# Reading all early expert rows at once, ahead of the next weight pieces, in a fused attention and expert-routing kernel

## The chip, the cores and the metric

The kernel runs on one core of a Trainium2 chip. The metric is the device time of one execution in microseconds; the kernel before was run three times. A separate execution under the hardware profiler gave the profile and the trace; all stretches and starts below are microseconds from the start of that profiled execution.

The engines go by these names: PE is TensorE (matmuls; PEld its weight loads), DVE is VectorE, ACT is ScalarE, POOL is GpSimd, SP is SyncE. In this kernel SP issues plain transfers (inputs, and the reads of routed rows), and POOL issues the indirect scatters and all weight transfers.

## The reference, cut to what matters

A linear attention without softmax, normalized per head, feeds a mixture of experts that sends each token to one expert:

```python
kv  = einsum('bhsd,bhse->bhde', k, v)             # 8 batches, 8 heads, 576 tokens, 64 wide
out = einsum('bhsd,bhde->bhse', q, kv)
out = out / sqrt(mean(out * out, -1) + 1e-6) * g_norm
x   = out.transpose(0, 2, 1, 3).reshape(4608, 512)
logits = x @ w_gate                                # 8 experts
e      = argmax(logits);  gate = softmax(logits)[e]
y[token] = gate * (relu(x[token] @ w1[e]) @ w2[e]) # w1: 512x1024, w2: 1024x512
```

## The kernel before: the parts that matter here

The tokens are worked in four pairs of batches (`j` = 0 to 3, nine tiles of 128 tokens each). For each tile TensorE makes the outputs (`o_mm`, tag `O`), ScalarE squares, VectorE reduces (`o_red`), ScalarE makes the reciprocal root (`o_nrm`), and VectorE scales into the row buffer `xrow` and the logits `lhat` (`o_x`), one tile behind. Every few tiles a `route` gives each token a slot in its expert's region of a DRAM table `x_slots`, and GpSimd scatters the rows there. Where a route is done in pieces (`chunks`), the last pieces are three tiles long.

```python
chunks = {0: [(0, 9)], 1: [(0, 9)], 2: [(0, 6), (6, 9)], 3: [(0, 3), (3, 6), (6, 9)]}
EARLY, EARLY_TILES = 3, 3

def route(j, t0, t1):                 # a generator: one step for each call of job()
    ...  # step 1: logits, maximum, one-hot (VectorE); ids into xrow (GpSimd)
    yield
    yield                             # step 2: nothing
    ...  # step 3: exp (ScalarE); ranks by matmul (rps, TensorE)
    yield
    ...  # step 4: positions, 1/sum (VectorE), then for each tile:
    for t in range(T):
        w = nc.gpsimd.indirect_dma_start(out=xs_views[9 * j + t0 + t], ...)   # scatter of rows
    yield
```

Experts 0, 1 and 2 have an early group each: the first 3 x 128 slots of the expert, which are filled from pairs 0 to 2 alone. After the last route of pair 2 a further job, `early_rows`, starts the reads of these groups. A group's rows are read by SyncE in four transfers of 96 KB, plus its gates and token ids (`gi`); such a read waits until the scatters have landed.

```python
def early_rows():
    ...                               # four small VectorE operations
    groups[0].fetch()
    yield
    yield
    groups[1].fetch()
    yield

def fetch(self):
    r0 = self.e * N + 128 * self.k0
    pool, bufs = (P_fe, 2) if self.table == "early" else (late["pool"], 3)
    self.xl = pool.tile([128, self.n // 32, 128], I16, tag="xl", bufs=bufs, name="xl")
    for i in range(4):
        r = nc.sync.dma_start(self.xl[32 * i : 32 * i + 32], ...)
        ...
    r = nc.sync.dma_start(self.gi[:, 0 : self.K], tail)
```

A group is then transposed and scaled on VectorE (`xpose`), and goes through `stage1` (eight times: four matmuls, ReLU on ScalarE into `hT`) and `stage2` (per 128 rows: eight matmuls into `yp`, gated on VectorE into `y`, scattered to the output by GpSimd). Early groups have three `y` buffers and two PSUM buffers each for `hp` and `yp`.

```python
def ffn():                            # one unit() = one stage1(f) or one stage2(k)
    to_fetch = list(groups[2:])
    ...
    for f in range(8):
        cur.stage1(f)
        ...
        if f == 1 or f == 5 and cur.K == SLOT_TILES:
            w_step()
        if f >= 4 and f % 2 == 0 and (f - 4) // 2 < parts:
            nxt.xpose((f - 4) // 2, parts)
        yield
    for k in range(cur.K):
        cur.stage2(k)
        if k % 2 == 1:
            w_step()
        ...
        yield
```

`w_step` issues the next of four weight pieces per expert on GpSimd's queue (two of w1, two of w2; float32 in DRAM, float16 in SBUF, 512 KB written each), in the order of the experts. After the attention `final_rows` starts pad scatters (`pads`, zero rows into unused slots), which GpSimd issues between the outputs, and which the reads of the later groups wait for.

The loop over the batches; `b` = 7 has pair 3's tiles 0 to 3, `b` = 8 (`B`) its tiles 4 to 8. A tile's `job()` calls run the waiting routes one step each.

```python
for n, t in enumerate(tiles):
    do_fill(1 if n == 0 and b < B else per - 1)
    job()
    tile_step(j, t)
    do_fill(1)
    o_nrm(j, t)
    job()
    if b == 6 and n >= 3 or b == 7 and n != 2 or b == B:
        w_step()
    if b == 7 and n == 3:
        w_step()
    if b == B and n >= 2:
        unit()
        unit()
```

Of the kernel before, what the change touches and what calls it, by code (L numbers as in the profile page):

```python
# [22 lines left out]
B, H, S, DH = 8, 8, 576, 64  # L23
# [11 lines left out]
EARLY = 3  # L35
# [10 lines left out]
def kernel(  # L46
# [94 lines left out]
    for j in range(4):  # L141
        for t0, t1 in chunks[j]:
            n = n_route
# [11 lines left out]
    P_fe = ctx.enter_context(tc.tile_pool(name="pearly", bufs=1))  # L155
# [13 lines left out]
    late = {}  # L169
# [61 lines left out]
    def id_index(name, ctr, ne, nk):  # L231
        badi = P_const.tile([128, ne, nk], I32, tag="badi" + name, name="badi" + name)
        nc.vector.tensor_tensor(
            badi, _bc(cv["srank"][:, 0:nk], 1, ne), _bc(ctr[:, 0:ne], 2, nk), op=ALU.is_ge
        )
        nc.vector.tensor_scalar(badi, badi, BIG, None, op0=ALU.mult)
        rows[name] = badi
# [5 lines left out]
    def disjoint(ins, others):  # L243
        for o in others:
            tc.declare_no_dep(ins, o, reason="other rows of the slots")


    def early_rows():
        ctr = P_const.tile([128, 8], F32, tag="cnt_x")
        b0 = base[len(routed)]  # L250
        nc.vector.tensor_tensor(ctr, b0, cv["ebase"], op=ALU.subtract)
        id_index("early", ctr, EARLY, EARLY_TILES)
        nc.vector.tensor_tensor(b0, b0, cv["efloor"], op=ALU.max)
        groups[0].fetch()
        yield
        yield
        groups[1].fetch()
        yield

    def final_rows():  # L260
# [6 lines left out]
    class Group:  # L267
# [28 lines left out]

        def fetch(self):
            r0 = self.e * N + 128 * self.k0
            pool, bufs = (P_fe, 2) if self.table == "early" else (late["pool"], 3)
            self.xl = pool.tile([128, self.n // 32, 128], I16, tag="xl", bufs=bufs, name="xl")  # L300
            for i in range(4):
                r = nc.sync.dma_start(
                    self.xl[32 * i : 32 * i + 32],
                    xs.ap()[r0 : r0 + self.n, 128 * i : 128 * i + 128].rearrange(
                        "(g b) w -> b g w", b=32
                    ),
                )
                disjoint(r.ins, [p for g, p in pad_ins if g is not self])
                read_ins.append(r.ins)
            self.gi = P_fe.tile([128, SLOT_TILES, 4], I16, tag="gi", bufs=4, name="gi")  # L310
            tail = xs.ap()[r0 : r0 + self.n, D:ROW].rearrange("(k p) w -> p k w", p=128)
            r = nc.sync.dma_start(self.gi[:, 0 : self.K], tail)
            disjoint(r.ins, [p for g, p in pad_ins if g is not self])
            read_ins.append(r.ins)
# [219 lines left out]
    groups = [Group(i, i, 0, EARLY_TILES) for i in range(EARLY)]  # L534
# [3 lines left out]
    def ffn():  # L538
        order = list(groups)
        side = []  # L540
        to_fetch = list(groups[2:])

        def fetch_up_to(n):
            while to_fetch and groups.index(to_fetch[0]) <= n:
                if to_fetch[0].table not in rows:
                    return
                to_fetch.pop(0).fetch()

        n = 0
        while n < len(order):  # L550
            cur = order[n]
            real = groups.index(cur) if cur in groups else -1
            nxt = groups[real + 1] if 0 <= real < len(groups) - 1 else None
            parts = 0 if nxt is None else 2 if nxt.K == SLOT_TILES else 1
            while w_todo and any(e == cur.e for e, _ in w_todo):
                w_step()
            if real == 0:
                cur.xpose()
            if real == EARLY:
                side.append(dyn_tables())  # L560
            for f in range(8):
                cur.stage1(f)
                if f == 0 and real >= 0:
                    fetch_up_to(real + (3 if real >= EARLY else 2))
                    if EARLY - 1 <= real < len(groups) - 4:
                        groups[real + 4].pads()
# [4 lines that stand above are left out]
                if f == 5:  # L571
                    cur.slot_ids()
                if f == 5 and cur.e == E - 1:
                    nc.gpsimd.drain()
                if f == 3 and cur.e == EARLY + 1:
                    spill = SpillGroup(tabs[0], slice(0, 1), out_views[E * SLOT_TILES])
                    spill.fetch()
                    n_more.append(
                        nc.values_load(
                            tabs[0][4][0:1, 0:1], min_val=0, max_val=MAXDYN - 1,  # L580
                            skip_runtime_bounds_check_because="the count of tiles is bounded",
                        )
                    )
                    order.insert(len(order) - 1, spill)
                for g in side:
                    next(g, None)
# [5 lines that stand above are left out]
                if k == 0 and real >= 0:  # L592
                    fetch_up_to(real + 2)
                if k == 3 and cur.e == E - 2:
                    spill.xpose()
                for g in side:
                    next(g, None)
                yield
            n += 1

    steps = ffn()

    def unit(n=1):
# [7 lines left out]
    with tc.tile_pool(name="pattn", bufs=1) as PA:  # L611
# [72 lines left out]
        def z_copy(b):  # L684
            zs[b] = PA.tile([128, 4, 64], F32, tag="z", bufs=2, name=f"z{b}")
            nc.scalar.copy(zs[b], kvps[b])
# [153 lines left out]
        def job():  # L840
            while jobs:
                try:
                    next(jobs[0])
                    return
                except StopIteration:
                    jobs.pop(0)
# [27 lines left out]
        for b in range(B + 1):  # L874
            fill = []
            if b < B:
                for u in range(2):
                    if b > 0:
                        fill.append(("kv", u))
                    for g in range(3 * u, 3 * u + 3):  # L880
                        fill.append(("t", g))
                    if b == 0:
                        fill.append(("kv", u))
                fill.append(("fold", 0))
            tiles = []
            if b > 0:
                j = (b - 1) // 2
                tiles = list(range(4)) if b % 2 else list(range(4, 9))
            per = (len(fill) + len(tiles) - 1) // len(tiles) if tiles else len(fill)

            def do_fill(n):
                for _ in range(n):
                    if not fill:
                        return
                    kind, x = fill.pop(0)
                    if kind == "kv":
                        kv_mm(b, x)
                        if b == 0:
                            load(2, x)
                        if x == 1:  # L900
                            z_copy(b)
                    elif kind == "t":
                        t_mm(b, x)
                        if x % 3 == 2:
                            if 0 < b < B - 2:
                                load(b + 2, x // 3)
                            if 2 * b + x // 3 in range(2, 2 + EARLY):
                                clear_early(2 * b + x // 3 - 2)
                    else:
                        fold_mm(b)  # L910
                        x_copy(b)

            if not tiles:
                do_fill(99)
# [4 lines that stand above are left out]
                do_fill(1)  # L919
                o_nrm(j, t)  # L920
                job()
                if b == 6 and n >= 3 or b == 7 and n != 2 or b == B:
                    w_step()
                if b == 7 and n == 3:
                    w_step()
                if b == B and n >= 2:
                    unit()
                    unit()
            do_fill(99)
# [49 lines left out]
```

## Time and profile before

| | |
|---|---|
| device time, three runs | 316.79, 319.02, 319.94 us; median 319.02 |
| profiled execution | 337.4 us, mean granted TensorE clock 0.888 |
| busy: PE, DVE, ACT, POOL | 268.3, 154.4, 121.3, 146.6 us |
| output matmuls of the attention (line 734) | to 160.0 us |
| first matmul of an early group (line 365) | at 152.3 us |

Three things help to read the views below. A timeline line is start, length, engine, source line, operation, what it writes and reads, how many were merged, and in brackets the idle time just before it with what ended it. SP lines (SPq) are issues, not transfers: the data moves later. In the table by stretch, each engine has its busy time and a count of instructions, and the last three numbers are the granted TensorE clock as a share of full speed, the mean busy share of the 16 DMA engines (it can come out a little over 1), and GB/s. The profiled execution is about 18 us longer than the timed ones; lengths in it are to be read with that in mind.

### The profile page before, as it was taken

The numbers are of one execution on the slowest core, as the hardware profiler recorded it, in microseconds if no ns is written. First come the engines' busy times: TensorE is split into PE (matmuls) and PEld (weight loads), VectorE is DVE, ScalarE is ACT, GpSimd is POOL, SyncE is SP. The second block draws the span as 40 slices with busy tenths as digits, with TensorE's granted clock in tenths as the row PEclk, the third lists the DMA queues.
The fourth block names the chain that finished last, engine by engine and source line by source line (L and its number), as shares of the span: only waits on it lengthen the run. The fifth ranks groups of instructions, "written<-read, shape, count | busy, mean of one in ns | idle before, by whom it ended". The sixth has DMA issues, their size and how long they took to land. (4 is left out here: it accounts for less than half of the span.)

```text
span 337.4 us, 6833 instructions
## 1 busy us (share of the span) xinstructions
PE 268.3 (80%) x2599; PEld 179.8 (53%) x2599; DVE 154.4 (46%) x397; ACT 121.3 (36%) x324; POOL 146.6 (43%) x186
## 2 busy tenths in 40 slices
PE   2789997399839849528597799779799999998991
PEld 1678785287628738424242355445446565654740
DVE  1015674137704645665661419775337282723031
ACT  2236664057505535323322043322414242332510
POOL 8400004600370074351457677777776362623132
PEclk9999999569955896757898799798999999999997
DMA  7999999939980329999922979999999997982012
GB/s 217 340 366 367 381 377 378 384 118 331 277 298 3 64 82 174 187 216 181 223 83 92 195 130 218 193 172 201 205 182 275 224 232 162 207 201 113 3 62 86
DMA packets 63346, 69.17 MB, mean 205 GB/s; under 512 B 31736, under 2 KB 48314, under 8 KB 63312
## 3 DMA queue, kind: packets, MB, share of 16 engines
q0 software_dynamic: 14496, 33.79, 44.8%
q1 hardware_dynamic: 48672, 34.79, 34.9%
q8 instruction: 21, 0.34, 0.4%
q10 hardware_dynamic: 144, 0.14, 0.4%
q14 instruction: 13, 0.11, 0.1%
HBM read 71.77 MB, written 20.79 MB: 274 GB/s over the span
## 5 line engine op out<-in xcount | busy, mean ns | idle before, releaser
L373 ACT ACTIVATE hT<-hp 128x320 f16<-128x320 f32 (+3 forms) x136 | 53.4, 426 | 114.2 <-PE hp L365 95.8
L365 PE MATMUL hp<-xT,w1e 128*128 128x320 f16 (+2 forms) x512 | 79.8, 309 | 15.7 <-DVE xT L327 7.0
L381 PE MATMUL yp<-w2e,hT 128*128 128x512 f16 x320 | 76.6, 397 | 4.6 <-DVE y L386 2.1
L365 PEld LDWEIGHTS <-w1e 128*128 128x128 f16 x512 | 51.1, 100 | 43.6 <-issue 22.5
L386 DVE TENSOR_SCALAR y<-yp,gi 128x512 f32<-128x512 f32 x40 | 29.8, 750 | 82.1 <-PE yp L381 75.8
L389 POOL DMA_INDIRECT out_dram<-y,idv x40 | 40.4, 1009 | 59.1 <-DVE y L386 44.9
L381 PEld LDWEIGHTS <-hT 128*128 128x128 f16 x328 | 32.9, 101 | 45.3 <-issue 9.8
L829 POOL DMA_INDIRECT x_slots<-xrow,posi x36 | 35.4, 983 | 49.9 <-issue 42.7
L734 PE MATMUL ops<-kvx,qT 64*128 64x72 f32 (+1 forms) x640 | 48.2, 302 | 4.9 <-issue 3.2
L747 DVE TENSOR_REDUCE ms<-sq 128x8 f32<-128x512 f32 x36 | 24.6, 684 | 58.7 <-ACT sq L743 49.9
L734 PEld LDWEIGHTS ops<-kvx,qT 64*128 64x128 f32 (+1 forms) x640 | 41.2, 205 | 12.7 <-issue 8.2
L677 PE MATMUL kvps<-mk,mv 128*64 128x64 f32 x640 | 31.8, 258 | 16.8 <-issue 11.8
L677 PEld LDWEIGHTS kvps<-mk,mv 128*64 128x64 f32 x640 | 27.5, 168 | 21.1 <-issue 18.9
L665 PE MATMUL tps<-ctile,mq 128*128 128x128 f32 x144 | 28.0, 331 | 12.3 <-DMA mq<-in_q_dram 6.3
L286 POOL DMA_INDIRECT x_slots<-zrow,padall x31 | 30.7, 989 | 9.4 <-issue 8.8
L743 ACT ACTIVATE sq<-ops 128x512 f32<-128x512 f32 x36 | 21.6, 599 | 35.1 <-PE ops L734 21.9
L759 DVE TENSOR_TENSOR xrow<-ops,rs 128x512 f16<-128x512 f32 x36 | 24.7, 685 | 14.3 <-ACT rs L752 12.9
L795 POOL COPY xrow<-tokc 128x3 int32<-128x3 int32 x12 | 2.4, 200 | 59.2 <-DVE xrow L759 59.2
L665 PEld LDWEIGHTS tps<-ctile,mq 128*128 128x128 f32 x144 | 18.5, 164 | 16.3 <-ACT qT L666 6.8
L666 ACT COPY qT<-tps 128x384 f32<-128x384 f32 x48 | 22.1, 473 | 12.1 <-PE tps L665 12.1
L322 DVE STREAM_TRANSPOSE xT<-xl 128x1280 int16<-128x1280 int16 (+2 forms) x16 | 24.0, 1503 | 2.7 <-DMA xl<-x_slots 2.7
L327 DVE TENSOR_SCALAR xT<-xT,g 128x320 f16<-128x320 f16 (+2 forms) x64 | 17.4, 335 | 0.6
(104 smaller groups left out, 140.9 us busy)
## 6 DMA issues: line engine op xcount, KB each, us to landing
mq<-in_q_dram SPq DMA_DIRECT2D x16, 576.0 KB
w1e<-in_moe_w_dram POOLq DMA_DIRECT2D x16, 512.0 KB
w2e<-in_moe_w_dram POOLq DMA_DIRECT2D x16, 512.0 KB
mk<-in_k_dram SPq DMA_DIRECT2D x16, 320.0 KB
mv<-in_v_dram SPq DMA_DIRECT2D x16, 320.0 KB
mk<-in_k_dram SPq DMA_DIRECT2D x16, 256.0 KB
mv<-in_v_dram SPq DMA_DIRECT2D x16, 256.0 KB
xl<-x_slots SPq DMA_DIRECT2D x20, 160.0 KB
```

Source lines behind the costliest of these rows:

```text
L286: p = nc.gpsimd.indirect_dma_start(out=self.pad_views[k], out_offset=IndirectOffsetOnAxis(ap=pad[:, self.e, self.k0 + k : self.k0 + k + 1] ...
L365: nc.tensor.matmul(hp, self.w()[0][:, kk].rearrange("p (m j t) -> p m t j", t=2, j=128)[:, f // 2, f % 2], self.xcols(kk, s), start=(kk == 0),
L373: nc.scalar.activation(self.hT[:, f, s : s + self.step], hp, ACTF.Relu)
L381: nc.tensor.matmul(yp, self.hT[:, f, k * 128 : (k + 1) * 128], self.w()[1][:, f // 2, f % 2, :], start=(f == 0), stop=(f == 7),)
L386: nc.vector.tensor_scalar(y, yp, self.gate(k), None, op0=ALU.mult)
L389: nc.gpsimd.indirect_dma_start(out=self.views(k), out_offset=IndirectOffsetOnAxis(ap=self.ids[:, k : k + 1], axis=0), in_=y, in_offset=Non ...
L665: nc.tensor.transpose(ps[:, c, :], src[:, 128 * m : 128 * m + 128], cv["ident"])
L677: nc.tensor.matmul(kvps[b][64 * y : 64 * y + 64, 2 * u + a, :], main["v", b, u][:, 2 * y + a, c, :], main["k", b, u][:, 2 * y + a, c, :], ...
L734: nc.tensor.matmul(ps[p0 : p0 + 64 * n, y, o0 : o0 + 72], qT[b][hs, a, blk // 2 : blk // 2 + n, :].rearrange("d c p -> d (c p)"), kvx[b][h ...
L747: nc.vector.reduce_sum(mss[j, t], sq, axis=AXX)
L759: nc.vector.tensor_tensor(xr[:, 0:D].bitcast(F16).rearrange("p (u y a d) -> p y u a d", u=2, y=2, a=2), xv.rearrange("p y (u a) d -> p y u ...
L829: w = nc.gpsimd.indirect_dma_start(out=xs_views[9 * j + t0 + t], out_offset=IndirectOffsetOnAxis(ap=posi[:, t : t + 1], axis=0), in_=xrow[ ...
```

## The change

The reads of all three early groups are issued together, in one step, right behind the last scatters of pair 2; the row buffer `xl` of the early groups gets a third copy so that they need not wait for each other. In `b` = 7 each tile runs three job steps instead of two, so the routes there are done sooner. The weight pieces that stood beside the reads (tile 3 of `b` = 7 had two, tile 0 of `b` = 8 one) are not issued there any more: by the end of the attention eight pieces have been issued instead of eleven, and the others follow with the groups. The units of the experts start one tile earlier (`n >= 1` in `b` = 8). It is meant to bring the first groups' rows in sooner, without weight transfers in their way.

```diff
@@ early_rows
-        groups[0].fetch()
-        yield
-        yield
-        groups[1].fetch()
+        for n in range(EARLY):
+            groups[n].fetch()
         yield
@@ Group.fetch
-            pool, bufs = (P_fe, 2) if self.table == "early" else (late["pool"], 3)
+            pool, bufs = (P_fe, 3) if self.table == "early" else (late["pool"], 3)
@@ ffn
-        to_fetch = list(groups[2:])
+        to_fetch = list(groups[EARLY:])
@@ the loop over batches
-                if b == 6 and n >= 3 or b == 7 and n != 2 or b == B:
+                if b == 6 and n >= 3 or b == 7 and n <= 1 or b == B and n >= 1:
                     w_step()
-                if b == 7 and n == 3:
-                    w_step()
-                if b == B and n >= 2:
+                if b == 7:
+                    job()
+                if b == B and n >= 1:
                     unit()
                     unit()
```

In the order of the instructions this moves the following. On GpSimd's queue the last scatters of pair 2 stand behind one w2 piece instead of two and ahead of one w2 piece instead of two w1 and one w2; expert 1's pieces stand behind the first scatters of pair 3, and expert 2's last piece behind the first pad scatters and five outputs. On VectorE the transpose of group 0 stands behind tile 5's reduction (before: behind tile 6's and a route's first step). On TensorE the last route's rank matmuls stand behind the first two outputs of group 0 (before: ahead of all three).

## The prediction

> **What bounds the kernel now.** I first read the shares on the page, then the table of busy time by stretch for the second half, then the waits of TensorE between 120 and 215 us, and last the timelines of SyncE, VectorE, GpSimd and TensorE round the longest of these waits. The chain of waits is of no use here: it ends after one piece, so the path has to be put together by hand. Rows of the stretches (start and end, length, busy time and count of PE, PEld, DVE, ACT, POOL, then granted clock, DMA share, GB/s):
> ```profile
> 118.00:138.40 20.40, 14.57 (x228) 12.36 (x223) 9.33 (x32) 8.40 (x23) 13.10 (x17) 0.83 0.66 140
> 138.40:152.30 13.90, 4.43 (x46) 4.03 (x38) 10.25 (x32) 3.83 (x12) 5.14 (x9) 0.52 1.08 198
> 152.30:163.80 11.50, 9.78 (x68) 5.48 (x67) 7.22 (x20) 5.43 (x14) 3.97 (x5) 0.84 1.05 192
> 249.00:300.00 51.00, 50.70 (x307) 29.91 (x306) 26.13 (x52) 18.37 (x48) 24.50 (x29) 1.00 1.02 218
> ```
> From 249 us on TensorE is busy for 50.7 of 51 us: a microsecond won ahead of this is kept if the feeders keep pace. The hole is 138.4 to 152.3: TensorE works 4.43 of 13.9 us, at a granted clock of 0.52, while the DMA share is 1.08. What ended its waits there (total, times, longest):
> ```profile
> PE hp L365 <- DVE xT L327: 7.0, 1, 7.0
> PE rps L806 <- DVE ohb L793: 4.6, 2, 2.8
> ```
> The 7.0 us are the first matmul of early group 0, which waits for its transposed rows. Who makes those rows late (SyncE's reads; GpSimd's scatters and weight pieces; VectorE's transpose):
> ```profile
> 139.81 2.66 SPq L302 DMA_DIRECT2D xl<-x_slots  x4
> 145.23 3.97 SPq L302 DMA_DIRECT2D xl<-x_slots  x4
> 135.43 0.97 POOL L829 DMA_INDIRECT x_slots<-xrow,posi  x1 [0.30 <-issue]
> 136.39 1.18 POOL L202 DMA_DIRECT2D w1e<-in_moe_w_dram  x2
> 137.66 0.75 POOL L207 DMA_DIRECT2D w2e<-in_moe_w_dram  x1
> 150.11 1.78 DVE L322 STREAM_TRANSPOSE xT<-xl 128x1536 int16<-128x1536 int16 x1 [1.69 <-DMA xl<-x_slots]
> ```
> Group 0's reads are issued at 139.81, once the last scatter of pair 2 (issued 135.43) has landed, and the transpose starts at 150.11: 10.3 us for 384 KB. Between lie three weight pieces, put on GpSimd's queue just ahead. The DMA view of 139.8 to 143.3 us has this queue line alone:
> ```profile
> q0 software_dynamic: 190, 0.71, 105.2%
> ```
> In the first 3.5 us after their issue no packet of the rows (queue 1) moved; the weights held all engines. From 143.3 to 146 the rows got 192 packets, and only from 146 to 152 the rest, two groups together.
>
> **What the Trainium skill says.** DMA: Bandwidth & Descriptors, section "Queues, rings and completion order", says that each DMA engine takes turns between the queues that have work, packet by packet. The trace agrees for 143.3 to 146 (223 weight packets beside 192 of rows): a 256-byte row packet waits its turn behind a 4 KB weight packet. TensorE: Matmul & The Clock Gate, "What's actually happening", says that an idle window of about 3.4 us halves the clock; the clock of 0.52 in the hole agrees, and the first group's 8 matmuls after it took 2.78 us where 8 later ones took 1.46. Perfetto Trace Analysis, "Tensor Engine Instruction", says that the profile's matmul ends are modelled; so I take group lengths by differences of starts.
>
> **The change part by part.**
>
> 1. *Reads without weights beside them.* Before, five weight pieces stand round pair 2's last scatters (two w2 ahead, two w1 and one w2 behind); after, one w2 ahead and one behind. Scatters: the routing step that makes their positions comes after tile 1's reduction instead of ahead of tile 2, about 1 us earlier (one `o_x` and one reduction, 0.69 + 0.26 + 0.69 us, fall behind it, less the wait for the reduction). Landing: before, the scatter packets stood behind two w2 pieces; a w2 piece is 256 packets of 0.173 us on 16 engines, 2.8 us, so some 1 us more is won. I put the reads at 138 us (139.81). Rows then meet one w2 piece at most. A later, undisturbed read shows the cost: group 3's reads were issued at 184.03 and mostly moved by 187.5 to 188. With 4 issues (2.66 us), some 3 us of packets and the completion, rows of group 0 land near 143.5 instead of 150.
>
> 2. *But the transpose is in VectorE's order.* The units start one tile earlier (`n >= 1`), so the transpose stands behind tile 5's reduction. Before, that reduction ran at 143.98 to 144.67; now the second half of a route (seven operations, 144.58 to 145.77: 1.2 us) stands ahead of it, but overlaps waits of 0.6 and 0.8 us. Transpose from about 144.8, then 1.78 and four scalings 1.27: rows ready at about 147.8. The first matmul moves from 152.3 to 147.8, **4.5 us**; the wait is not gone, about 5 us of it is left, so the clock stays low there.
>
> 3. *What was moved behind it.* Tile 6's output matmuls (about 1.1 to 1.5 us) were done ahead of 152.3 and now come behind: **-1.3 us**. In return, the 2.8 us wait of TensorE at 163.8 to 166.6 for the last route's one-hot goes: in the new order the first two outputs of group 0 (16 matmuls, 3.5 us) stand ahead of that route's matmuls. **+2.8 us.** Sum at group 1's first matmul: 4.5 - 1.3 + 2.8 = 6.0 us (173.3 to about 167.3).
>
> 4. *Weights come later against the compute.* Three pieces fewer are issued by the end of the attention (8 instead of 11); every later piece slips by about one early group. Expert 1: four pieces issued at about 147 to 151; at 2.6 us (w1: 128 packets of 0.325 us on 16 engines) and 2.8 us each they take 11 us, landed by about 162, wanted at 167: hidden. Expert 2's last w2 piece is the tight one. It now stands in GpSimd's queue behind the last three scatters, six pad scatters and outputs 4 and 5. An indirect scatter takes 0.98 us and 0.30 between: 1.29 each. The last scatters end at about 174.3 (176.1 before: they stand behind three outputs now); a w2 piece 0.8; six pads 7.8, to 183; two outputs 2.6; the piece ends its issue at 186.6 and lands some 4 us later (2.8 of packets), at 190.5. TensorE, 6 us early, wants it after group 1 (two stages, 6.4 + 5.2 as group 2's starts at 191.61, 197.99 and 203.16 show), group 2's first stage (6.4) and four matmuls: 167.3 + 18.0 + 0.9 = 186.2. **A new wait of about 4.3 us, over half of the gain.**
>
> 5. *GpSimd's queue.* From 176 to 249 us it runs nearly back to back (43.66 of 58 us busy from 191 to 249, plus 0.3 between each two). It decides when `y` buffers (three in the early groups) come free. Its end of the first pads moves from 186.4 to about 183, 3 us, so it can't pass on much more than that. Weights for experts 3 to 7 keep over 15 us between issue and use: expert 4's, issued 213 to 228 before, are wanted at 254.
>
> 6. *The third row buffer* removes group 2's wait for a free buffer (its reads went out at 153.48, right after group 0's transpose ended, for a transpose at 175): hidden before, worth nothing.
>
> Sum: 6.0 - 4.3 = 1.7 us by TensorE's path, about 3 us by GpSimd's; and if the wait for the weights is missing, up to 6. I choose **3 us: 316.0**, nearer to the lower two. One caution: the profiled execution took 337.4 us, the timed ones 319. In the profile TensorE's results come 3 to 5 us late at several places (VectorE waited 10.0 us for the first output of group 1, until 188.31), and I counted group lengths there from undisturbed groups.
>
> **The rivals.**
> - *The bound passes fully to the weights or to GpSimd.* If the pads and outputs end no earlier, expert 2's last piece and the `y` buffers eat all 6 us: 319, or 321 if DMA traffic makes the piece land 2 us later still. For it: the unbroken GpSimd queue, and the DMA share of 1.00 from 191 to 249. Against: the last scatters do come earlier.
> - *The hole closes further and the weights arrive in time.* With the DMA engines quiet (share 0.48 from 173.3 to 191 before) the piece may land sooner, and a shorter hole may leave the clock at full: then 6 to 7 us, 312 to 313.
> - *The read was hidden anyway.* If VectorE or the clock, not the rows, set the start of group 0, the gain is 1 us. Against: the 1.69 us wait of the transpose for the rows just ahead of 150.11, after which nothing else was missing.
>
> **Range and chances.** The terms that pull against each other are each some 3 us uncertain; the three times before spread over 3.2 us. Range 311.5 to 320.0. Over 2% faster needs under 312.6, the second rival nearly whole: 0.15. Over 2% slower needs 325.4: 0.04. Within 2%: 0.81.
>
> **What would show it.** (a) Group 0's rows issued at about 138 and its transpose about 5 us earlier than 150.1; (b) a wait for xT of about 5 instead of 7.0 us; (c) no wait of 2.8 us for the one-hot ahead of group 0's outputs; (d) a wait in group 2's second stage for expert 2's w2, some 2 to 4 us, or none, if I am wrong on the weights; (e) the first pads end about 3 us sooner; (f) from group 3 on the same lengths. Wrong would I be above all if (d) is absent (then faster) or if the later weights are missed again at expert 3 (then slower).

## The result and the profile after

The kernel before took 317.90 us in this comparison (median of 4 runs, 316.76 to 319.94), the changed one **306.06 us** (4 runs, 305.54 to 307.45). The ratio is 0.9627, with an interval of 0.9559 to 0.9695: 12 us gained, where 3 were foretold. The execution under the profiler has a span of 304.1 us.

The waits of TensorE from 90 to 200 us in the changed kernel (total, times, longest, in us):

```profile
PE yp L379 <- DMA w2e<-in_moe_w_dram: 7.3, 1, 7.3
PE hp L363 <- DVE xT L325: 6.8, 2, 6.6
PE rps L804 <- DVE ohb L791: 3.7, 2, 2.9
```

The wait for group 0's rows (`xT`) is 6.6 us and the new wait for expert 2's `w2` is there, 7.3 us. By these lines alone the change should have lost: 7.0 before against 6.6 + 7.3 now. What answers to the reads and the weight pieces in the timelines of SyncE, GpSimd and VectorE (start, duration, engine, tiles, count, and in brackets the idle time before):

```profile
114.83 2.04 SPq L300 DMA_DIRECT2D xl<-x_slots  x4
117.43 2.14 SPq L300 DMA_DIRECT2D xl<-x_slots  x4
120.21 2.20 SPq L300 DMA_DIRECT2D xl<-x_slots  x4
...
109.20 0.77 POOL L207 DMA_DIRECT2D w2e<-in_moe_w_dram  x1
120.37 1.18 POOL L202 DMA_DIRECT2D w1e<-in_moe_w_dram  x2
123.45 1.43 POOL L207 DMA_DIRECT2D w2e<-in_moe_w_dram  x2
...
119.73 1.78 DVE L320 STREAM_TRANSPOSE xT<-xl 128x1536 int16<-128x1536 int16 x1 [2.35 <-DMA xl<-x_slots]
```

All three groups' reads are issued within 8 us, the next weight pieces come behind those of the first, and the transpose starts 4.9 us after its reads are issued (10.3 before). But these starts are 25 to 30 us earlier than those of the profile before (139.81 and 150.11), which no part of the change can do: the attention ahead of them is the same work. Here lies the key to the missing 9 us. The profiled execution of before took 337.4 us, the timed ones 317 to 319. In it TensorE crept in the attention; the stretch from 57 to 70 us (busy time and count of PE, PEld, DVE, ACT, POOL, then granted clock, DMA share, GB/s), first in that execution:

```profile
57.00:70.00 13.00, 6.67 (x56) 4.46 (x58) 2.24 (x4) 2.59 (x7) 6.84 (x8) 0.63 0.92 335
```

and in a second profile of the same kernel, whose execution took 315.76 us (run e13_before below):

```profile
57.00:70.00 13.00, 12.37 (x247) 10.92 (x248) 8.55 (x18) 9.25 (x27) 6.71 (x10) 1.00 1.06 387
```

56 matmuls against 247 in the same 13 us, with the same scatters on GpSimd beside them. This second profile is the one to compare with. Its waits of TensorE from 90 to 200 us, its hole as a stretch, its timelines, and the DMA queues from 119 to 130 us (packets, MB, share):

```profile
PE hp L365 <- DVE xT L327: 26.6, 1, 26.6
PE rps L806 <- DVE ohb L793: 4.2, 2, 2.8
PE yp L381 <- DVE y L386: 3.5, 1, 3.5
...
110.70:137.30 26.60, 0.03 (x2) 0.06 (x2) 5.06 (x15) 1.11 (x3) 5.75 (x8) 0.50 1.04 198
...
106.47 1.18 POOL L202 DMA_DIRECT2D w1e<-in_moe_w_dram  x2
107.74 0.74 POOL L207 DMA_DIRECT2D w2e<-in_moe_w_dram  x1
115.58 0.77 POOL L207 DMA_DIRECT2D w2e<-in_moe_w_dram  x1
116.45 1.16 POOL L202 DMA_DIRECT2D w1e<-in_moe_w_dram  x2
...
115.38 2.96 SPq L302 DMA_DIRECT2D xl<-x_slots  x4
121.99 12.17 SPq L302 DMA_DIRECT2D xl<-x_slots  x4
...
135.09 1.78 DVE L322 STREAM_TRANSPOSE xT<-xl 128x1536 int16<-128x1536 int16 x1 [21.30 <-DMA xl<-x_slots]
...
q0 software_dynamic: 866, 2.27, 96.7%
q1 hardware_dynamic: 820, 0.20, 13.4%
```

**The hole is 26.6 us long, not 7.0**, and TensorE does nothing in it (0.03 us busy). The reads go out at 115.38, in the midst of the weight pieces, and the transpose waits until 135.09. The two DMA lines show why: in 11 us GpSimd's queue (q0: the weights, and 0.40 MB of scattered rows) moved 866 packets and the read rows' queue (q1) 820, nearly one for one, but 2.27 MB against 0.20. The second group's four issues on SyncE alone took 12.17 us. In the changed kernel the same two queues from 116 to 121 us read:

```profile
q1 hardware_dynamic: 3109, 0.67, 79.7%
q0 software_dynamic: 85, 0.25, 12.8%
```

3,109 packets on the rows' queue in 5 us, beside 85, of which 60 are scattered rows and one is of weights.

### The profile page after: what moved, and what is told of

It reads as the page before. It is cut to its first block, busy times and chain, and to the rows that moved or that the text cites. A ratio compares the mean times of both kernels' runs of the same rounds, so it can differ in the third digit from the quotient of the medians.

```text
span 304.1 us, 6828 instructions
## 1 busy us (share of the span) xinstructions
PE 256.4 (84%) x2599; PEld 173.5 (57%) x2599; DVE 153.1 (50%) x397; ACT 120.4 (40%) x324; POOL 147.1 (48%) x186
## 5 line engine op out<-in xcount | busy, mean ns | idle before, releaser
L379 PE MATMUL yp<-w2e,hT 128*128 128x512 f16 x320 | 74.9, 390 | 9.4 <-DMA w2e<-in_moe_w_dram 7.3
L732 PE MATMUL ops<-kvx,qT 64*128 64x72 f32 (+1 forms) x640 | 45.9, 296 | 1.6 <-issue 1.1
L732 PEld LDWEIGHTS ops<-kvx,qT 64*128 64x128 f32 (+1 forms) x640 | 40.1, 202 | 7.8 <-issue 4.4
L663 PE MATMUL tps<-ctile,mq 128*128 128x128 f32 x144 | 27.1, 322 | 7.0 <-DMA mq<-in_q_dram 5.5
L675 PE MATMUL kvps<-mk,mv 128*64 128x64 f32 x640 | 25.6, 244 | 7.1 <-DMA mv<-in_v_dram 5.6
L741 ACT ACTIVATE sq<-ops 128x512 f32<-128x512 f32 x36 | 21.6, 600 | 22.1 <-PE ops L732 21.3
L675 PEld LDWEIGHTS kvps<-mk,mv 128*64 128x64 f32 x640 | 23.3, 156 | 9.7 <-issue 6.5
L664 ACT COPY qT<-tps 128x384 f32<-128x384 f32 x48 | 22.1, 473 | 10.9 <-PE tps L663 10.9
L663 PEld LDWEIGHTS tps<-ctile,mq 128*128 128x128 f32 x144 | 18.1, 161 | 11.2 <-DMA mq<-in_q_dram 5.2
L749 ACT ACTIVATE rs<-ms,epsb 128x8 f32<-128x8 f32 x36 | 10.8, 301 | 18.4 <-DVE ms L745 17.9
```

The source lines that it names most:

```text
L379: nc.tensor.matmul(yp, self.hT[:, f, k * 128 : (k + 1) * 128], self.w()[1][:, f // 2, f % 2, :], start=(f == 0), stop=(f == 7),)
L663: nc.tensor.transpose(ps[:, c, :], src[:, 128 * m : 128 * m + 128], cv["ident"])
L675: nc.tensor.matmul(kvps[b][64 * y : 64 * y + 64, 2 * u + a, :], main["v", b, u][:, 2 * y + a, c, :], main["k", b, u][:, 2 * y + a, c, :], ...
L732: nc.tensor.matmul(ps[p0 : p0 + 64 * n, y, o0 : o0 + 72], qT[b][hs, a, blk // 2 : blk // 2 + n, :].rearrange("d c p -> d (c p)"), kvx[b][h ...
```

## The experiments

The change has three parts, tried alone and in pairs. In the tables and headings below they are R, W and J:

```diff
R (reads)    -        groups[0].fetch(); yield; yield; groups[1].fetch()
             +        for n in range(EARLY): groups[n].fetch()      # and bufs 2 -> 3
W (weights)  -                if b == 6 and n >= 3 or b == 7 and n != 2 or b == B:
             -                    w_step()
             -                if b == 7 and n == 3:
             +                if b == 6 and n >= 3 or b == 7 and n <= 1 or b == B and n >= 1:
J (steps)    -                if b == B and n >= 2:       # before unit(); unit()
             +                if b == 7:
             +                    job()
             +                if b == B and n >= 1:       # before unit(); unit()
```

### First, in the creeping condition

The first eight runs all fell where TensorE crept as in the profile given: the kernel before took 338 us there in 110 executions. They do not bear on the timed 12 us, but they show what the change is worth with that timeline. First the kernel before itself, and each part alone.

> The kernel before, unchanged, profiled again. If the long profile of before (337.4 us against 319 timed) was one odd execution, this one has a span near 317 and the pauses of 10 us at 59 and at 90 us, where the instructions are those of the changed kernel, are gone; then the 27 us by which the changed kernel's profile is ahead at that point are no part of the change. If the pauses belong to this program, the profile is again near 337 us with pauses at the same places. Time: 1.00 of before either way.

> Only the reads: all three early groups read in one step, with a third row buffer; weight pieces, job steps and units as before. Theory A (the weight pieces beside the reads make the rows late): the reads still wait behind three pieces, so 0 to 1 us faster at most. Theory B (what counts is that reads are issued together): most of the 12 us, near 0.965. Theory C (the gain is outside the hole, in the attention part, through another placement of buffers that comes with the third row buffer): also most of the 12 us, but with the hole at the first group as long as before, about 7 us.

> Only the weight pieces: issued as in the changed kernel (eight by the end of the attention, none beside the reads), reads, buffers, steps and units as before. Theory A: rows of group 0 land about 6 us sooner, but units start a tile later than in the change; 3 to 8 us faster (0.975 to 0.99). Theory B and C: 0 to 1 us, or slower by the wait for expert 2's last w2 piece (up to 7 us).

> Only the steps: three job steps per tile in batch 7 and units from the second tile of batch 8 on; weights and reads as before (so group 1's reads come right after group 0's). Theory A: the wait for group 0's rows stays, since the weights are still in the way: 0 to 3 us faster, the 2.8 us wait for the last one-hot goes. Theory B: 0 to 1 us.

Measured, with before at 337.90: before again 338.40, reads alone 340.35 (ratio 1.0137, 1.0045 to 1.0228), weights alone 337.76 (0.9977, 0.9939 to 1.0014), steps alone 336.16 (4 runs, 330.14 to 340.47). TensorE's longest wait for `xT` was 7.8 us in before, 9.2 with the reads, 5.3 with the weights and 8.9 with the steps. The weights alone shorten the wait here, as the prediction had it, but the 3 to 8 us expected of them are not in the time, and the reads alone are not faster at all. Then all three parts and the pairs, with before at 338.35.

> The whole change, beside the kernel before on one chip. On the chip of the four runs above the kernel before takes 338 us and TensorE crawls (a few matmuls each 1.4 us) while GpSimd issues its indirect scatters one behind the other; the profile of the change has none of that. Theory D (the crawl is a matter of the chip or of the moment, not of the change): the change shows the crawl too wherever the kernel before is near 338, and its true gain is 0.96 to 0.98. Theory E (the change itself ends the crawl): near 306 beside 338, a ratio of 0.90 to 0.92.

> Reads together and weights out of their way, but two job steps per tile in batch 7 and units from the third tile of batch 8 on, as before. Theory A (rows without weights beside them): group 0's rows land about 6 us sooner, but are used a tile later; 2 to 6 us faster than before. Theory B (only the steps bring it): 0 to 1 us.

> Weights out of the way and the three steps, but reads 0 and 1 in steps of their own, group 2's read later, two row buffers. Theory A: nearly the whole gain, within 1 us of the full change, since the third buffer and the joint reads hide nothing. Theory B (reads together count): less than half of the gain.

> Reads together and the three steps, but the weights as before, eleven pieces by the end of the attention with three beside the reads. Theory A: most of the gain is missing, group 0's rows land near where they did before, 0 to 3 us faster. Rival: expert 2's last w2 piece is there in time, no wait of 7 us in group 2's second stage, so the whole is as fast as the full change.

Measured: the whole change 335.92 (0.9949, 0.9914 to 0.9985), R + W 337.46 (0.9989, 0.9943 to 1.0036), W + J 336.91 (0.9934, 0.9894 to 0.9975), R + J 339.40 (0.9926, 0.9880 to 0.9973; here the ratio leaves out the disturbed ones of 22 executions, which the plain median holds). The change crept as well, so it is not what ends the creeping. With that timeline the whole change wins **2.4 us** at the median, close to the 3 foretold. In part that is luck: the wait for `xT` is 4.0 us where about 5 was foretold, but the wait for `w2`, which was to cost 4.3 us, is not there. The prediction described the execution that it was read from, and that was not one like those that were timed. What set it apart in the hole: the attention ended at 138.4 instead of 110.7 us, and the weights that GpSimd issues beside it probably had more time to move. Only 0.65 MB were still on their way on GpSimd's queue among the first 1,536 row packets (one group's 384 KB), against 2.62 MB in the second profile.

### Then, as timed

The kernel before again, to see whether the hole is longer where TensorE does not creep:

> The kernel before, once more, for a profile of an execution like those that gave the median of 318 us. If 338 us of the eight runs above is a condition of the moment, this one may be near 318, and then shows where the 20 us lie: by the theory of the crawl, in the stretches where GpSimd issues indirect scatters back to back (9 + 9 in the attention, the pads after it), and nowhere else. If it is near 338 again, the comparison of the parts has to be made under that condition.

The wait for `xT` was **26.8 us**. This execution took 324.91 us, above the median of the kernel, so the profile was repeated later, beside the single parts:

> The kernel before once more, one look. Theory of the hole: where TensorE does not crawl in the attention, its first matmul of group 0 waits 20 us or more for xT, as in the last look (26.8), and the execution takes about 317. Rival (that look was slower than the median by chance in this place): a wait of 15 us or less.

26.6 us, in an execution of 315.76. The long hole is typical. Now the parts, on the same footing. Weights alone, and in pairs:

> Only the weight pieces moved, reads, buffers and steps as before. In the kernel before, executed without the crawl, TensorE waits 26.8 us for group 0's rows, because the reads stand beside seven queued pieces. Theory F (the pieces beside the reads are nearly the whole of it): that wait falls to below 12 us and the time to within 4 us of the full change, 306 to 311. Theory G (steps or joint reads carry it): 314 to 318 with a wait over 18 us.

> Weights and steps, but the reads one by one and two row buffers. Theory F: as fast as the full change, 305 to 308, since groups 1 and 2 are wanted only after group 0. Theory G (joint reads count): 310 or more.

> Joint reads, third buffer and steps, the weight pieces as before. Theory F: the wait for group 0's rows stays above 20 us; 315 or more, no gain, or slower, as more rows compete. Theory G: 306 to 310.

Then steps and reads alone, and the third pair:

> The steps alone (three routing steps per tile in batch 7, units from tile 1 on), the weight pieces and the two-stage reads as before. Theory that only the pair (fewer weight pieces, earlier steps) closes the hole: the wait for xT stays at 18 to 26 us, time 308 to 317. Rival, the steps are the whole of it: wait of 8 us or less, 304 to 307.

> The reads alone (all three groups at once, three row buffers), weights and steps as before. Theory: the hole stays (20 to 28 us, three groups now share the queues with the weights, so group 0's rows land no earlier), time 314 to 322. Rival, the joint read is what gains: 306 to 310 and a wait of 10 us or less.

> Reads and weights, no steps. Theory that only the pair of weights and steps closes the hole: the wait for xT is 18 to 24 us as with the weights alone, time 308 to 316, with a wait of 4 to 8 us for w2. Rival, reads before the weights need only these two parts: wait of 8 us or less, 304 to 307.

All of them, each against the kernel before on the same chip: its median was 316.05 us beside R, J and R + W, 317.38 beside W, W + J and R + J, and 317.90 beside the change. "Weights among rows" is counted from the trace's packets: the bytes that GpSimd's queue moved between the first and the 1,536th packet of the early rows, and the time between the two. Up to 0.40 MB of these bytes are scattered rows of pair 3, the rest is weights.

| parts | run | us (median) | ratio, interval | wait for xT, longest | wait for w2, total | weights among rows, time |
|---|---|---|---|---|---|---|
| none | e13_before | 316.05 | 1 | 26.6 | none | 2.62 MB, 13.7 us |
| R | e15_reads | 316.33 | 0.9986, 0.9876 to 1.0096 | 26.1 | none | 2.64 MB, 13.6 us |
| W | e9_weights | 310.68 | 0.9735, 0.9645 to 0.9825 | 21.9 | 8.2 | 2.09 MB, 13.4 us |
| R + W | e16_reads_weights | 313.35 | 0.9917, 0.9833 to 1.0001 | 19.9 | 4.6 | 1.23 MB, 7.7 us |
| J | e14_steps | 305.63 | 0.9613, 0.9512 to 0.9714 | 13.0 | none | 0.62 MB, 4.1 us |
| R + J | e11_reads_steps | 307.36 | 0.9645, 0.9570 to 0.9721 | 22.1 | none | 2.13 MB, 11.2 us |
| W + J | e10_weights_steps | 304.10 | 0.9601, 0.9503 to 0.9700 | 7.1 | 8.5 | 0.13 MB, 2.8 us |
| R + W + J | the change | 306.06 | 0.9627, 0.9559 to 0.9695 | 6.6 | 7.3 | 0.04 MB, 2.9 us |

Three things follow.

**The steps alone win as much as the whole change**: 0.9613 beside 0.9627, each known to about 1 per cent from four executions. My theory for that run (a wait of 18 to 26 us, 308 to 317 us) fell; its rival, that the steps are the whole of it, held in the time, and in the wait only half (13.0 us, not 8). The waits of TensorE from 125 to 301 us and the timelines of the kernel with the steps alone:

```profile
PE hp L365 <- DVE xT L327: 16.2, 3, 13.0
...
107.30 1.15 POOL L202 DMA_DIRECT2D w1e<-in_moe_w_dram  x2
117.25 1.53 POOL L207 DMA_DIRECT2D w2e<-in_moe_w_dram  x2
118.73 0.60 POOL L202 DMA_DIRECT2D w1e<-in_moe_w_dram  x1
...
112.78 2.78 SPq L302 DMA_DIRECT2D xl<-x_slots  x4
```

The reads go out 2.6 us earlier than in the second profile of before (112.78 against 115.38), and the next weight pieces 1.7 us later (117.25 against 115.58), behind three scatters that come 1.7 us later as well. So the rows meet one batch of pieces that is nearly through, and move in a gap between two batches. TensorE starts group 0 at 125.3 instead of 137.3, 12.0 us earlier, and the span is 301.5 instead of 314.1, 12.6 shorter: the net gain is won at that start. J holds two edits, the third job step in batch 7 and the units one tile earlier, and they were not tried apart. The trace speaks for the job step: VectorE stands idle for 21.3 us ahead of the transpose in before, waiting for the rows alone, so units that come earlier could not start it sooner, while the reads go out 0.5 us after TensorE's last attention matmul instead of 4.7.

**Taking the weights away from the reads shortens the hole further, but the time stays the same.** With W and J the wait for `xT` falls to 7, but expert 2's second `w2` piece comes 7 to 9 us late. The start of group 3 shows the exchange: with J alone it comes 44.7 us after group 0's first matmul (170.0 less 125.3), in the changed kernel 55.3 (177.2 less 121.9). The 3.4 us won at the start are more than given back there. From group 3 to the end the change is then 4.6 us shorter (126.9 against 131.5); the steps alone have 3.2 us of waits for the next groups' rows there, the change 0.3.

**The joint reads and the third buffer are worth nothing measurable** (R alone 0.9986; W + J without R is no slower than with it). R + W even stands behind W, 0.9917 beside 0.9735, but on another chip; no run settles that.

The wait follows the bytes among the rows all the way, from 2.6 MB and 26 us down to 0.04 MB and 6.6 us; R + W stands somewhat above the others: without the steps its reads go out 4.7 us after TensorE's last attention matmul (119.48 after 114.8), and the first row packet moves another 3.7 us later (123.16). One thing stays open: W and R + J still show waits of about 22 us and yet gain 7 to 10 us at the median. Each trace is of one execution, and these two were the longest of their sets (317.52 and 313.82, R + W too with 317.78), those of J and W + J the shortest (303.18 and 296.14). The hole in the other executions may well lie between; there is no trace of those.

### A better version

If the remaining loss is the late `w2`, one more weight piece per tile, put behind the reads, should win it back. The change with this addition (a second piece in each tile of batch 8 from the third on, so that the loop issues 11 pieces instead of 8; the twelve in the text below count one more, which the first group issues in both kernels):

```diff
                 if b == 6 and n >= 3 or b == 7 and n <= 1 or b == B and n >= 1:
                     w_step()
+                if b == B and n >= 2:
+                    w_step()
```

> The full change, with a second weight piece in each of the last three tiles of batch 8, once the early rows have landed: twelve pieces by the end of the attention instead of eight. In the change TensorE waits 7.3 us for expert 2's second w2 piece. If that wait is on the path: it is gone and the time is 3 to 7 us below the change, 299 to 303. If the pieces only push the scatters of pair 3 back, or the wait for the next rows (group 3, behind the pads) takes its place: 0 to 2 us.

Measured **296.60 us** (295.67 to 297.49), ratio 0.9315 (0.9240 to 0.9389) against before, below the interval of the change (0.9559 to 0.9695). That is 9.5 us below the change, more than the 3 to 7 expected. Its waits of TensorE from 90 to 200 us and the weight pieces on GpSimd:

```profile
PE hp L363 <- DVE xT L325: 15.2, 3, 10.2
PE rps L804 <- DVE ohb L791: 4.7, 4, 3.0
PE hp L363 <- ACT hT L371: 1.5, 1, 1.5
...
124.60 1.43 POOL L207 DMA_DIRECT2D w2e<-in_moe_w_dram  x2
126.01 1.11 POOL L202 DMA_DIRECT2D w1e<-in_moe_w_dram  x2
139.80 1.55 POOL L207 DMA_DIRECT2D w2e<-in_moe_w_dram  x2
```

Expert 2's two `w2` pieces are issued at 139.80 instead of 151.89 and 163.01, and the wait for `w2` is gone, though the one for group 0's `xT` is 3.6 us longer than in the change. Group 3 starts 40.9 us after group 0 (164.0 less 123.1), against 55.3 in the change and 47.2 in the second profile of before (184.5 less 137.3). Of these 14.4 us the late `w2` accounts for 7.3, and for 2.4 more in which TensorE ran at the low clock after that wait. The other 4.6 lie ahead of group 1, where the granted clock was 0.89 instead of 0.59 (step 2 below); whether the added pieces or the one execution made that difference, no run shows. From group 3 on 4.9 us go back: two new waits for the next groups' rows (3.5 and 1.5 us) take the place of the one for `w2`, as the last clause of the expectation feared.

## Why the prediction was wrong, step by step

**What bounds it: right in place and kind, wrong in size.** The rows of group 0 are what TensorE waits for, and weights in the queues are why. The wait was put at 7.0 us; where the times were taken it is 26.6. The prediction's caution named the mismatch of 337.4 and 319 us, but took it to lie in later groups only, and counted every term from the crept timeline.

**Step 1, the failed step.** "Rows of group 0 land near 143.5 instead of 150", 6.5 us, counted from a read that met 0.65 MB of weights. With the 2.62 MB of the second profile a working by bytes gives the right order: 2.27 MB moved in 11 us is 206 GB/s, so 2.62 MB take 12.7 us, and 13.7 were measured, against 2.9 without weights. The transpose starts at 119.73 instead of 135.09, **15.4 us** earlier. The earlier scatters won their part too: before, the reads went out 4.7 us after TensorE's last attention matmul (115.38 less 110.7), in the changed kernel 0.5 us ahead of it (the hole starts at 115.3). The shares were wrong too: the step gave the earlier scatters about 2 us (reads at 138 instead of 139.81) and the absence of weights the rest, but J, which leaves the weight pieces where they stood in the loop, starts group 0 12.0 us earlier, while W still shows a wait of 21.9 us in its one trace. Trainium skill, DMA: Bandwidth & Descriptors, section "Queues, rings and completion order" (turns by packet), was cited for a stretch of 2.7 us, where most of the weight packets were of 2 KB (176 of 207), not 4 KB; the 866 and 820 packets agree with it over 11 us.

**Step 2, the order of VectorE.** It was to hold the transpose back; in the changed kernel the 2.35 us ahead of the transpose are a wait for the rows (`xl`). The first matmul moved from 137.3 to 121.9, 15.4 us, not 4.5. That some 5 us of the wait stay was right (6.6), and so was the low clock. The stretch from the first matmul of group 0 to that of group 1:

```profile
121.90:145.50 23.60, 22.61 (x112) 12.38 (x112) 13.51 (x41) 7.23 (x19) 7.00 (x10) 0.59 0.80 147
```

The granted clock is 0.59, and this is where the trace and the page part. Trainium skill, TensorE: Matmul & The Clock Gate, "What's actually happening", has the clock halved after an idle window, which agrees with the 0.50 in the hole; but it has the full clock back after about 3.4 us of sustained work. In before it was back 3.2 us after the first matmul (at 140.5). In the changed kernel it stayed at 0.50 from 121.9 to 141.0, though TensorE was busy for 18.11 of these 19.1 us. Two lots of eight matmuls of that time (in before such eight took 1.48 us at 144.68 and 1.46 at 147.12):

```profile
126.48 2.74 PE L363 MATMUL hp<-xT,w1e 128*128 128x384 f16 x8
136.91 2.74 PE L363 MATMUL hp<-xT,w1e 128*128 128x384 f16 x8
```

It stayed low as long in R + J (19 us), for 8 us with the steps alone, and for 3 and 8 us in two profiles of before. What decides it stays open; it costs the changed kernel's profile some of what the shorter hole won.

**Step 3, -1.3 and +2.8.** The one-hot wait behind group 0 is gone, as foretold; the 2.9 us left of it stand ahead of the hole, at 109.7. But the stretch got 2.9 us longer (23.6 against 20.7), not 1.5 shorter: TensorE is busy for 22.61 us of it, before for 16.22. The outputs of one more tile (16 matmuls, 1.99 us) and the low clock outweigh the wait. From 15.4, 12.4 us are left at group 1's first matmul (157.97 to 145.55), where 6.0 were foretold.

**Step 4, the late `w2`: right, but too small.** Foretold were 4.3 us, measured 7.3. TensorE's timeline and GpSimd's issue:

```profile
162.25 1.03 PE L379 MATMUL yp<-w2e,hT 128*128 128x512 f16 x4
170.59 4.81 PE L379 MATMUL yp<-w2e,hT 128*128 128x512 f16 x11 [7.31 <-DMA w2e<-in_moe_w_dram]
...
163.01 0.79 POOL L207 DMA_DIRECT2D w2e<-in_moe_w_dram  x1
```

The piece is issued at 163.01, just as TensorE wants it, behind the scatters, pads and outputs named. The matmul runs 6.8 us after the issue's end, where 4 were taken: that is the mis-sized term. Over half of the gain was to go there; of 12.4 us at group 1, 7.3 are left at group 3 (184.5 to 177.2), the 3.5 us wait for a `y` buffer that fell away counted.

**Step 5, GpSimd.** The first pads end at about 160.4 instead of 171.1, 10.7 us sooner, not 3, so the limit that the step saw in GpSimd was not there. From group 3 to the end the changed kernel takes 126.9 us against 129.6 (304.1 less 177.2, 314.1 less 184.5): by point (f) these were to be the same, and no run explains the 2.7 us. The sum closes: 7.3 + 2.7 = 10.0 us of span, where the medians differ by 11.8.

**Step 6, the third buffer: right**, worth nothing.

**The rivals.** "The hole closes further" came nearest, with the wrong half: the hole closed by 20 us, and the weights were not in time. Neither "fully eaten" nor "hidden anyway" held. What the named cause of the change does is another matter: the steps, which I took for a means, bring the time, and the weights kept away, which I took for the means, bring nothing measurable on top of them.

## What to carry to other kernels

Compare the span of a profile with the timed runs first; where they differ by more than the effect that is sought, every term read from the trace is of another timeline, and a wait behind a queue that drains meanwhile is the first to be false. Small transfers that a consumer waits for should be issued into a gap of a queue of large ones; count the bytes that will stand among them, and price these at the measured rate. Keeping large pieces away is only half of it: say where they go instead, since here 7 us came back at expert 2 until its pieces were issued earlier, behind the reads.

## What the runs showed of the hardware that was not expected

- In some executions TensorE crept while GpSimd issued its scatters, and the kernel before took 338 us instead of 317. From 92 to 104 us of the profile given (72 matmuls, 5.08 us busy of 12) TensorE's timeline has pieces like these, where the profile names no releaser:

```profile
97.75 0.50 PE L677 MATMUL kvps<-mk,mv 128*64 128x64 f32 x4 [0.91 <-issue]
99.20 0.39 PE L677 MATMUL kvps<-mk,mv 128*64 128x64 f32 x3 [0.95 <-issue]
101.31 0.47 PE L677 MATMUL kvps<-mk,mv 128*64 128x64 f32 x3 [1.14 <-issue]
```

  One and the same chip showed it in one set of runs and not in a later one, and the scatters have the same durations and gaps (0.97 and 0.30 us) in both. Its cause stays open; nothing was tried on it.
- Where weight packets filled the DMA engines, a read's first packet moved 3.5 us after its issue (115.38 to 118.89 in before, with 253 weight packets in that time; 112.78 to 116.31 with the steps alone, with 182). With 17 of them it moved after 1.0 us (114.83 to 115.81 in the change).
- After the hole TensorE's granted clock came back after 3 us of work in some profiles and after 19 in others (step 2 above).
